# A block-diagonal state for one tile shape in linear attention, and a new order of jobs, in a fused mixer kernel on one core

## The chip, the core and the metric

The kernel runs on one core of a Trainium2 chip. The core has a matrix engine (TensorE, PE in the rows; its weight loads are PEld), a vector engine (DVE), a scalar engine (ACT), GpSimd (POOL) and SyncE (SP), which here only issues transfers. Each engine works through its own queue in order. The metric is the device time of one execution in microseconds (us); smaller is better.

## The reference

Three layers follow one another, for a batch B of 2 and a sequence S of 768. Inputs are float32, the weights are float64.

```python
# 1: linear attention with decay, 8 heads of D = 64
state = gamma * state + einsum('bhd,bhe->bhde', k[:, :, t], v[:, :, t])
y[:, :, t] = scale * einsum('bhd,bhde->bhe', q[:, :, t], state)
# 2: Fourier mixing, then a normalised MLP of 512 -> 2048 -> 512
u = x + real(fft(fft(x, axis=1), axis=2))
un = (u - mean(u)) / sqrt(var(u) + 1e-6)
x = u + relu(un @ w_ch1) @ w_ch2
# 3: 512 -> 1024, a gate from a convolution over 3 tokens, 1024 -> 512
h = relu(x @ w_in)
out = (h * sigmoid(conv3(h)) @ w_out)
```

## The kernel before

The whole program is a list of small jobs, one string `ORDER`. Each engine gets its instructions in the order of that string; nothing is reordered afterwards, so a job that waits holds everything behind it on the same engine. The names that matter here:

- Attention works on 12 tiles n of 128 tokens, 0 to 5 for the first batch, 6 to 11 for the second. `Lk`, `Lq`, `Lv` load one input tile each (256 KB, from the SP queue unless `ACT_LOADS` names it). `V` scales v by the decay (POOL, DVE if in `V_DVE`, ACT if in `V_ACT`). `K` and `Q` transpose k and q on PE, and ACT copies them out. `S` makes the scores on PE, and DVE masks them (L265). `A` adds the tile to the state (L276), and ACT copies the sums out (L279). `O` makes the output: the product with the state of the tiles before (L299), then the product of scores and v (L302); ACT copies it out. `X` transposes it back (L312), and DVE scales it to rows (L317); from the fourth tile of a batch on, SP writes the rows to DRAM as well.
- Fourier mixing: `F` and `G` fold each row block (two small instructions each; `F` on POOL unless in `FOLD_DVE`, `G` on DVE). `b0.0` to `b0.9` are the butterflies over the six blocks of a batch, 14 instructions of 128x512 (DVE, some on POOL unless in `FLY_DVE`). `t` transforms over tokens and `p` over features on PE; `m` and `r` add the results to u; `rev` gathers rows back from DRAM (POOL queue).
- `s`, `n`, `x` are the moments, the centring and the transposes of the MLP's input. `U00.f` and `D00.f` are its up and down products for batch 0, first half of the tokens, chunk f; `h` and `P` are the third layer's products.
- Weights arrive as float64 halves of chunks, 48 in all: `f` fetches 512 KB into one of three raw buffers, `d` decodes it to float32 with three DVE instructions (L507, L509, L511), `e` splits it into two parts (ACT L501; L503 on POOL if in `LOW_POOL`, else DVE).

The tile shapes on PE, rows by columns of the array: transposes and all MLP products use 128x128, the scores 64x128 (two heads in the two halves of the rows), the state 128x64 (two heads in the two halves of the columns), the product with the state 64x64, the value product 128x64. The state of the eight heads lies in a PSUM bank as 128 x 256: head 2hp+j in partitions 64j to 64j+63, columns 64hp to 64hp+63.

Of the kernel before, what the change touches and what calls it, by code (L numbers as in the profile page):

```python
# [42 lines left out]
ORDER = """
clear warm Lk0 ident K0 Lq0 Q0 masks S0 Lv0 V0 A0 Lk2 K2 Lq1 Q1 Lk1 K1 Lv1 V1 Lq2 Lv2 V2 O0 Lq3 Lq6 S1 Lk3 Q2 Lq4 A1
X0 F0 G0 O1 A2 Lv3 V3 S2 K3 Q3 X1 Q4 F1 G1 O2 A3 S3 Lk4 K4 Lk5 K5 Lv4 V4 X2 F2 S4 Lq5 Q5 Lk6 Lv6 V6 G2 Lv5 V5 Lv7 V7
f1 Lk7 Lq7 O3 K6 A4 X3 Q6 Lq8 F3 S5 f0 d1 Lk8 G3 b0.0 b0.3 O4 K7 X4 Q7 F4 S7 Lq9 G4 O5 X5 Q8 A6 A7 K8 F5 O7 d0 e0 G5
b0.2 b0.5 S6 O6 b0.1 b0.8 b0.9 b0.4 b0.6 b0.7 f2 d2 e1 Lk10 K10 f5 d5 tables t0.4 t0.0 t0.1 f3 d3 e2 rev0 e3 S8 t0.2
f4 d4 f6 d6 t0.3 p0.2 p0.0 m0.0 s00.0 n00.0 m0.2 p0.1 m0.1 s00.1 n00.1 s00.2 x00.0 X7 e6 n00.2 x00.1 x00.2 f8 e5 e4 f7
d7 Lk9 Lv8 V8 A8 Lk11 X6 Q9 K9 r0.0 U00.0 s01.0 r0.1 U00.1 s01.1 n01.1 d8 dev00 rec00 n01.0 Lv10 D00.0 U00.3 Lq10 Q10
F6 G6 Lv9 V9 x01.0 O8 Lv11 V11 K11 A9 f9 e7 r0.2 s01.2 dev01 rec01 U00.2 S9 x01.1 D00.1 V10 n01.2 x01.2 Lq11 O9 A10  # L50
f10 d10 e8 F7 G7 f11 d11 e11 U01.1 X9 F9 X8 F8 Q11 D00.2 D00.3 Z00.4.2 Z00.4.1 d9 e9 S10 U01.0 f23 U01.3 O10 f13 d13
f12 e10 d12 f15 G8 D01.0 Z00.4.0 U01.2 e12 d15 e15 G9 X10 F10 G10 b1.1 S11 D01.1 D01.2 U00.5 U00.4 e13 f14 d14 O11
b1.0 b1.3 f16 d16 f17 f18 D00.4 X11 F11 D01.3 Z01.4.0 Z01.4.2 b1.4 U00.6 G11 b1.2 U01.4 Z01.4.1 e14 d17 f20 e16 d18
f19 b1.5 D00.5 D00.6 Z00.7.0 U00.7 Z00.7.2 U01.5 Z00.7.1 b1.8 b1.9 b1.6 b1.7 e18 d19 f21 e17 d20 f22 D01.4 D01.5 U00.8
U01.6 t1.2 e20 d21 f24 t1.1 t1.0 e19 d22 e22 e21 d23 t1.4 D01.6 Z01.7.1 Z01.7.0 U00.9 t1.3 D00.7 D00.8 p1.1 rev1 d24
e24 m1.1 p1.2 m1.2 r1.2 f26 r1.1 Z01.7.2 U00.11 U00.10 d26 f31 e23 D00.9 U00.12 e26 f27 d27 e27 f25 d25 e25 f28 d28
D00.10 D00.11 U00.13 p1.0 e28 m1.0 s10.0 r1.0 s11.0 U01.7 D00.12 D00.13 U01.9 U01.8 n10.0 f32 s10.2 n10.2 f29 d29 e29
d31 e31 s10.1 D01.7 U01.10 s11.2 f30 d30 e30 D01.8 U01.11 d32 s11.1 D01.9 U01.12 D01.10 D01.11 U00.14 U00.15 x10.0
n10.1 dev11 rec11 f33 d33 D00.14 D00.15 Z00.16.2 Z00.16.1 U01.14 U01.13 x10.1 x10.2 n11.1 f38 f39 f36 n11.0 conv
Z00.16.0 dev10 rec10 D01.12 D01.13 D01.14 U10.2 U10.0 U10.1 D10.0 D10.1 U01.15 U10.3 D01.15 Z01.16.1 Z01.16.2 U10.5  # L60
Z01.16.0 x11.0 D10.2 U10.4 D10.3 U10.7 x11.1 n11.2 D10.4 D10.5 U10.6 U10.10 D10.6 U10.8 D10.7 D10.8 U10.9 U10.13 D10.9
D10.10 U10.11 U10.12 D10.11 U10.15 x11.2 D10.12 U11.2 D10.13 U10.14 y00.0 y00.1 D10.14 D10.15 Z10.16.0 Z10.16.1
Z10.16.2 U11.0 U11.1 D11.0 e33 d39 e32 d36 f34 U11.3 f35 D11.1 D11.2 e36 d34 e34 d35 U11.4 U11.5 D11.3 U11.7 D11.4
U11.6 e39 d38 e38 f37 d37 e37 f42 d42 y00.2 D11.5 D11.6 e42 D11.7 U11.10 U11.8 U11.9 e35 f40 d40 e40 f44 d44 f41 d41
e44 e41 D11.8 D11.9 U11.12 U11.11 f46 d46 f45 d45 e45 D11.10 U11.13 D11.11 h00.0 f47 d47 e47 f43 d43 e43 e46 D11.12
D11.13 U11.15 U11.14 y01.0 y01.1 y01.2 D11.14 D11.15 Z11.16.1 Z11.16.2 Z11.16.0 h01.0 c0.0 a0.0 h01.1 h00.1 c0.1 h01.2
h00.2 c0.2 h00.3 w0.0 y10.0 a0.2 w0.2 a0.1 h00.5 y10.1 h00.4 h01.3 c0.3 w0.1 h01.5 c0.5 a0.3 h01.4 c0.4 a0.4 h00.6
h01.7 y10.2 w0.4 w0.3 h00.7 y11.0 y11.1 y11.2 h01.6 c0.6 a0.5 w0.5 h10.2 a0.6 w0.6 h10.0 c0.7 a0.7 h10.1 w0.7 h11.1
c1.1 h11.0 c1.0 a1.0 w1.0 h10.3 h11.2 c1.2 a1.2 h11.6 w1.2 h10.6 P0.2 P0.3 a1.1 w1.1 h10.4 h11.3 c1.3 a1.3 w1.3 h10.7
h11.7 h11.4 c1.4 a1.4 c1.6 a1.6 h10.5 h11.5 P0.1 P0.4 c1.5 a1.5 P0.0 w1.5 w1.4 w1.6 c1.7 P0.5 a1.7 w1.7 P1.1 P1.0 P1.2  # L70
P1.4 P1.3 P1.5
"""


# [709 lines left out]
```

## Time and profile before

| | |
|---|---|
| Time, median of 3 runs | 528.16 us (527.57 to 528.64) |
| Time of the profiled execution | 527.51 us |
| Span of the profiled execution | 525.6 us (1.9 us of its time lie around the span) |
| PE busy | 506.1 us, 96% of the span |
| DVE busy | 322.9 us, 61% |
| ACT, POOL busy | 172.0 us, 66.0 us |
| Chain that ended last | 93% PE, 3% DVE, 1% DMA |

The span runs from the first instruction to the last. Engine time is how long the engine had an instruction at work; the chain is the work that ended last, followed back from the end. The shares are means over the whole span; the rows further down take single stretches of it.

### The profile page before, as it was taken

The page shows a single profiled execution, that of the slowest core. Times are in us where ns is not written, and L with a number is a line of the kernel's source. Part 1 is how long each engine was busy: PE and PEld are TensorE (multiplying, and loading weights), DVE is VectorE, ACT ScalarE, POOL GpSimd, SP SyncE. Part 2 cuts the span into 40 slices and gives each one's busy share as a digit, 9 for nine tenths or more (in the row PEclk, how much of TensorE's full clock was granted, in tenths as well). Part 3 has the DMA queues.
Part 4 walks back from the last instruction along what each step waited for, and adds up shares of the span by engine and source line. Part 5 has one row for each costly group of instructions (what it writes and reads, how often), then busy time and mean ns, then how long its engine had stood idle before and what let it go on. Part 6 is the DMA issues. An engine that isn't in the chain of part 4 may idle for free.

```text
span 525.6 us, 7790 instructions
## 1 busy us (share of the span) xinstructions
PE 506.1 (96%) x3182; PEld 453.9 (86%) x3182; DVE 322.9 (61%) x576; ACT 172.0 (33%) x336; POOL 66.0 (13%) x66
## 2 busy tenths in 40 slices
...
GB/s 194 204 239 257 179 103 81 162 96 87 174 107 143 157 104 58 126 76 2 0 1 0 1 0 1 148 94 134 67 2 0 1 1 1 41 0 61 40 40 61
DMA packets 60951, 42.59 MB, mean 81 GB/s; under 512 B 42098, under 2 KB 55026, under 8 KB 60916
## 3 DMA queue, kind: packets, MB, share of 16 engines
...
q8 instruction: 25, 0.41, 0.3%
...
q14 instruction: 10, 0.08, 0.1%
...
## 4 chain that ended last, share of the span: by engine, by line
PE 93%; DVE 3%; DMA 1%; ACT 1%; SPq 1%; issue 0%; ACTq 0%
PE h L136 9%; PE ac L136 9%; PE h L138 9%; PE h L137 9%; PE ac L138 9%; PE ac L137 8%; PE hi L138 4%; PE hi L137 4%; PE hi L136 4%; PE po L136 4%; PE po L138 4%; PE po L137 4%; PE sc L263 2%; PE px L302 2%; PE tr L579 2%; PE px L299 2%
## 5 line engine op out<-in xcount | busy, mean ns | idle before, releaser
L609 DVE SCALAR_TENSOR_TENSOR h<-h,h 128x384 fp32r<-128x384 f32 x64 | 35.2, 554 | 88.9 <-ACT h L608 88.9
L136 PE MATMUL ac<-wt,h 128*128 128x512 f32 x192 | 76.9, 400 | 0.0
L608 ACT ACTIVATE h<-h 128x384 fp32r<-128x384 f32 x64 | 31.2, 490 | 137.4 <-PE h L138 132.6
L138 PE MATMUL ac<-wt,h 128*128 128x512 f32 x192 | 75.8, 395 | 0.0
L137 PE MATMUL ac<-wt,h 128*128 128x512 f32 x192 | 75.5, 393 | 0.0
L503 POOL TENSOR_TENSOR wt<-word,wt 128x512 fp32r<-128x512 f32 x18 | 23.3, 1296 | 227.4 <-ACT wt L501 227.4
L501 ACT CAST wt<-word 128x512 fp32r<-128x512 f32 x48 | 29.0, 619 | 56.3 <-DVE word L511 53.7
L138 PEld LDWEIGHTS ac<-wt,h 128*128 128x128 f32 x192 | 36.1, 188 | 8.6 <-DVE h L609 0.3
L136 PEld LDWEIGHTS ac<-wt,h 128*128 128x128 f32 x192 | 36.1, 188 | 7.0 <-issue 0.3
L137 PEld LDWEIGHTS ac<-wt,h 128*128 128x128 f32 x192 | 36.1, 188 | 6.7
L136 PE MATMUL po<-wt,g 128*128 128x512 f32 (+1 forms) x104 | 39.1, 376 | 0.0
L138 PE MATMUL po<-wt,g 128*128 128x512 f32 (+1 forms) x104 | 39.0, 375 | 0.0
L137 PE MATMUL po<-wt,g 128*128 128x512 f32 (+1 forms) x104 | 39.0, 375 | 0.0
L667 DVE SCALAR_TENSOR_TENSOR cv<-hb,cw,cv 128x768 f32<-128x768 f32 x32 | 32.5, 1017 | 10.5 <-ACT cv L665 9.9
L511 DVE SCALAR_TENSOR_TENSOR word<-raw,word 128x512 int32<-128x512 int32 x48 | 34.6, 721 | 1.6
L509 DVE SCALAR_TENSOR_TENSOR word<-raw,word 128x512 int32<-128x512 int32 x48 | 33.7, 703 | 1.6
L507 DVE TENSOR_SCALAR word<-raw 128x512 int32<-128x512 int32 x48 | 21.6, 450 | 8.1 <-POOL wt L503 7.7
L696 DVE COPY ob<-po 128x512 f32<-128x512 f32 (+1 forms) x13 | 8.3, 648 | 29.4 <-PE po L138 29.4
L503 DVE TENSOR_TENSOR wt<-word,wt 128x512 fp32r<-128x512 f32 x30 | 20.4, 688 | 8.9 <-ACT wt L501 8.7
L138 PEld LDWEIGHTS po<-wt,g 128*128 128x128 f32 x104 | 19.5, 188 | 3.8
L137 PEld LDWEIGHTS po<-wt,g 128*128 128x128 f32 x104 | 19.6, 188 | 3.7
L136 PEld LDWEIGHTS po<-wt,g 128*128 128x128 f32 x104 | 19.5, 188 | 3.7
...
## 6 DMA issues: line engine op xcount, KB each, us to landing
...
```

The lines of the kernel that those rows point to most:

```text
L136: nc.tensor.matmul(o, ah, bh, start=start, stop=False)
L137: nc.tensor.matmul(o, ah, bl, start=False, stop=False)
L138: nc.tensor.matmul(o, al, bh, start=False, stop=stop)
L263: nc.tensor.matmul(ps[j][:, sl], kt[rows, sl], qt[rows, sl], start=True, stop=True)
L501: nc.scalar.copy(wt[:, 0, j], f32(word))
L503: eng.tensor_tensor(wt[:, 1, j], f32(word), f32(wt[:, 0, j]), op=ALU.subtract)
L507: nc.vector.tensor_scalar(word, raw[:, :, 1], 3, 0x3FFFFFF8, op0=ALU.logical_shift_left, op1=ALU.bitwise_and)
L509: nc.vector.scalar_tensor_tensor(word, raw[:, :, 1], -0x40000000, word, op0=ALU.bitwise_and, op1=ALU.bitwise_or)
L511: nc.vector.scalar_tensor_tensor(word, raw[:, :, 0], 29, word, op0=ALU.logical_shift_right, op1=ALU.bitwise_or)
L608: nc.scalar.activation(h2[:, 0], ps[:, :HB], AF.Relu)
L609: nc.vector.scalar_tensor_tensor(h2[:, 1], ps[:, :HB], 0.0, f32(h2[:, 0]), op0=ALU.max, op1=ALU.subtract)
L667: nc.vector.scalar_tensor_tensor(cv, hb[:, j:j + S], f32(cw[:, j * NF2 + f:j * NF2 + f + 1]), cv, op0=ALU.mult, op1=ALU.add)
```

## The change

The state is stored block-diagonally: for each pair of heads a 128 x 128 block in which head j fills rows and columns 64j to 64j+63, and the rest is zero, set once at the start (one more clearing instruction, on POOL). The product with the state then takes all 128 rows of q and the zeros fall out, so `A`, and both products of `O`, use the shape 128x64. ACT copies the state out in two instructions in place of one. The states take the place of one work buffer, which moves to the last of the spare tiles, and the q tiles of the second batch have one buffer in place of two.

The order is new throughout, and with it the lists that say which engine takes a job. Two loads (`q0`, `v1`) go out from the ACT queue in place of one. The fetches `f2` and `f0` stand behind six input tiles; seven fetches stand ahead of `Lv5`, where there was none. The part of the new and old order up to the last attention job is shown; the rest (second half of the first MLP and the third layer) is regrouped in the same way.

```diff
-V_ACT = ()
+V_ACT = (4,)
 V_DVE = (5, 6, 10)
-FOLD_DVE = (0, 9)
-FLY_DVE = ((0, 0), (0, 1), (0, 2), (0, 8))
-BACK_DVE = ((0, 2), (1, 0))
-LOW_POOL = (0, 3, 6, 7, 9, 12, 15, 18, 24, 27, 30, 31, 33, 36, 38, 39, 42, 45)
-WORD_BANK = (5, 37, 43)
-CENTRE_ACT = ((0, 0, 0), (0, 0, 2), (0, 1, 0), (0, 1, 2), (1, 0, 0), (1, 0, 2), (1, 1, 0))
-ACT_LOADS = ('k0',)
+FOLD_DVE = (0, 3, 5, 10)
+FLY_DVE = ((0, 0), (0, 1), (0, 8), (1, 8))
+BACK_DVE = ((1, 0),)
+LOW_POOL = (0, 3, 6, 7, 9, 12, 14, 15, 16, 18, 24, 25, 27, 30, 31, 33, 36, 39, 42, 43)
+WORD_BANK = (5, 19, 40, 45, 47)
+CENTRE_ACT = ((0, 0, 0), (0, 0, 2), (0, 1, 0), (0, 1, 2), (1, 0, 1), (1, 0, 2))
+ACT_LOADS = ('q0', 'v1')
 ORDER = """
-clear warm Lk0 ident K0 Lq0 Q0 masks S0 Lv0 V0 A0 Lk2 K2 Lq1 Q1 Lk1 K1 Lv1 V1 Lq2 Lv2 V2 O0 Lq3 Lq6 S1 Lk3 Q2 Lq4 A1
-X0 F0 G0 O1 A2 Lv3 V3 S2 K3 Q3 X1 Q4 F1 G1 O2 A3 S3 Lk4 K4 Lk5 K5 Lv4 V4 X2 F2 S4 Lq5 Q5 Lk6 Lv6 V6 G2 Lv5 V5 Lv7 V7
-f1 Lk7 Lq7 O3 K6 A4 X3 Q6 Lq8 F3 S5 f0 d1 Lk8 G3 b0.0 b0.3 O4 K7 X4 Q7 F4 S7 Lq9 G4 O5 X5 Q8 A6 A7 K8 F5 O7 d0 e0 G5
-b0.2 b0.5 S6 O6 b0.1 b0.8 b0.9 b0.4 b0.6 b0.7 f2 d2 e1 Lk10 K10 f5 d5 tables t0.4 t0.0 t0.1 f3 d3 e2 rev0 e3 S8 t0.2
-f4 d4 f6 d6 t0.3 p0.2 p0.0 m0.0 s00.0 n00.0 m0.2 p0.1 m0.1 s00.1 n00.1 s00.2 x00.0 X7 e6 n00.2 x00.1 x00.2 f8 e5 e4 f7
-d7 Lk9 Lv8 V8 A8 Lk11 X6 Q9 K9 r0.0 U00.0 s01.0 r0.1 U00.1 s01.1 n01.1 d8 dev00 rec00 n01.0 Lv10 D00.0 U00.3 Lq10 Q10
-F6 G6 Lv9 V9 x01.0 O8 Lv11 V11 K11 A9 f9 e7 r0.2 s01.2 dev01 rec01 U00.2 S9 x01.1 D00.1 V10 n01.2 x01.2 Lq11 O9 A10
-f10 d10 e8 F7 G7 f11 d11 e11 U01.1 X9 F9 X8 F8 Q11 D00.2 D00.3 Z00.4.2 Z00.4.1 d9 e9 S10 U01.0 f23 U01.3 O10 f13 d13
-f12 e10 d12 f15 G8 D01.0 Z00.4.0 U01.2 e12 d15 e15 G9 X10 F10 G10 b1.1 S11 D01.1 D01.2 U00.5 U00.4 e13 f14 d14 O11
-b1.0 b1.3 f16 d16 f17 f18 D00.4 X11 F11 D01.3 Z01.4.0 Z01.4.2 b1.4 U00.6 G11 b1.2 U01.4 Z01.4.1 e14 d17 f20 e16 d18
+clear warm Lq0 ident Lk0 K0 Q0 masks S0 Lv1 Lv0 Lk1 Lq1 V0 A0 K1 Q1 O0 f2 f0 Lk2 d2 d0 S1 K2 X0 Lq3 F0 G0 V1 O1 A1 Lv3
+e2 X1 V3 Lq2 Q2 S2 Lk3 K3 Q3 Lv2 V2 O2 A2 f1 d1 Lv6 V6 F1 f5 d5 Lk4 e0 Lv4 V4 X2 F2 S3 O3 f3 d3 G1 K4 Lq4 Q4 Lq5 Lq6
+G2 Lk5 A3 f6 Lk7 Lk6 f4 X3 F3 G3 Q6 Lq7 S4 b0.0 b0.3 Lv7 Lv5 Lk8 e3 d6 A4 tables Q5 K5 V7 e1 d4 O4 K7 S5 V5 K6 X4 Q7
+Lq8 F4 S7 G4 O5 A6 Lk9 K8 X5 F5 G5 b0.2 A7 Lk10 f10 S6 O6 K9 f7 b0.5 b0.1 b0.8 b0.9 b0.4 b0.6 b0.7 Q8 S8 Lq9 e4 d7 O7
+e6 e5 X6 Q9 t0.0 t0.3 t0.2 t0.1 t0.4 p0.1 m0.1 p0.0 m0.0 s00.0 s00.1 n00.0 n00.1 Lv10 f8 Lv9 V9 p0.2 m0.2 s00.2 Lv8 V8
+A8 O8 A9 f11 x00.0 n00.2 x00.1 X7 Lk11 K10 x00.2 rev0 Lv11 V11 S9 F6 Lq10 Q10 Lq11 K11 r0.1 s01.1 n01.1 U00.0 r0.2
+s01.2 U00.1 r0.0 s01.0 dev01 rec01 n01.0 V10 S10 F7 e7 G7 U00.2 x01.0 x01.1 n01.2 d11 f13 dev00 rec00 d8 f9 G6 e8 d10
+D00.0 D00.1 D00.2 e11 f15 O10 O9 A10 U00.3 x01.2 e10 X8 F8 Q11 d9 e9 f12 G8 X9 F9 D00.3 Z00.4.0 Z00.4.1 U01.0 U01.1 G9
+X10 F10 G10 b1.1 U01.2 Z00.4.2 d12 e12 f23 d13 S11 d15 e15 b1.4 b1.0 D01.0 D01.1 D01.2 U00.5 U01.3 U00.4 O11 f16 d16
+b1.3 f14 f20 e13 d14 f18 D00.4 U00.6 X11 F11 G11 b1.2 D01.3 Z01.4.1 Z01.4.2 Z01.4.0 U01.4 e14 d18 f24 b1.5 e16 d20 f17
...
-    sums = [states[:, 0, i * 256:(i + 1) * 256] for i in range(2)]
+    sums = [states[:, i, :].rearrange("p (a e) -> p a e", a=NP) for i in range(2)]
...
-    parts = [p[:, i, :] for p in parts for i in range(4)] + [states[:, 1, :]]
+    spare = [slot(9, [P, 4, H, D], "spare0"), uslot(1, 1, [P, 3, H, D], "spare1", F32)]
+    parts = [p[:, i, :] for p in parts for i in range(4)] + [spare[1][:, 2].rearrange("p h d -> p (h d)")]
...
-        return spare[6 + n % 2] if n >= NC else kv_late[4 + n % 2]
+        return spare[6] if n >= NC else kv_late[4 + n % 2]
...
+        nc.gpsimd.memset(states[:, 1, :], 0.0)
...
-                nc.tensor.matmul(st[j * D:(j + 1) * D, hp * D:(hp + 1) * D], k_tile(n)[:, 2 * hp + j, :],
+                nc.tensor.matmul(st[j * D:(j + 1) * D, hp * P + j * D:hp * P + (j + 1) * D], k_tile(n)[:, 2 * hp + j, :],
...
-        nc.scalar.copy(sums[(c + 1) % 2], st[:, 0:256])
+        for j in range(2):
+            sl = slice(j * D, (j + 1) * D)
+            nc.scalar.copy(sums[(c + 1) % 2][sl, :, sl], st[sl, :].rearrange("p (a e) -> p a e", a=NP)[:, :, sl])
...
-                rows = slice(j * D, (j + 1) * D)
-                nc.tensor.matmul(place(h), sums[c % 2][rows, hp * D:(hp + 1) * D], qt[rows, hp * P:(hp + 1) * P],
+                nc.tensor.matmul(place(h), sums[c % 2][:, hp, j * D:(j + 1) * D], qt[:, hp * P:(hp + 1) * P],
```

## Rows read from the trace of the kernel before

**Rows 1.** Windows of 10 us: length, busy us of PE, PEld, DVE, ACT, POOL (instructions), clock, DMA.

```profile
40.00:50.00 10.00, 7.81 (x118) 6.28 (x116) 8.01 (x14) 3.78 (x9) 3.58 (x4) 1.00 0.80 226
50.00:60.00 10.00, 5.03 (x32) 4.51 (x29) 9.62 (x16) 2.44 (x5) 3.01 (x3) 0.79 0.62 207
70.00:80.00 10.00, 4.76 (x33) 3.97 (x33) 9.15 (x22) 4.28 (x9) 4.04 (x4) 0.81 0.38 97
80.00:90.00 10.00, 10.00 (x65) 9.16 (x64) 7.60 (x16) 5.34 (x10) 3.41 (x4) 0.85 0.52 107
```

**Rows 2.** Timeline: last butterfly; first mix; last centring; first up product.

```profile
55.81 0.69 DVE L383 TENSOR_TENSOR fold<-fold,fold 128x512 f32<-128x512 f32 x1
...
70.66 0.43 DVE L457 TENSOR_TENSOR mix<-pc,mix 128x258 f32<-128x258 f32 x1 [0.35 <-ACT mix L434]
...
78.64 0.72 ACT L556 ACTIVATE un<-u,ve 128x512 f32<-128x512 f32 x1 [2.75 <-DVE ve L535]
...
83.53 0.42 PE L136 MATMUL h<-un00h,wt 128*128 128x384 f32 x1
```

**Rows 3.** Chain that ended last, 20 to 32 us: start us, us, engine and line.

```profile
20.90 1.02 PE px L299 x16
21.92 1.02 PE px L302 x16
22.94 0.47 PE st L276 x16
23.41 1.09 PE sc L263 x16
...
30.27 0.61 PE st L276 x16
...
31.47 0.44 PE pq L252 x4
```

**Rows 4.** The page's groups of a decode: count | busy us, mean ns | idle before.

```profile
L511 DVE SCALAR_TENSOR_TENSOR word<-raw,word 128x512 int32<-128x512 int32 x48 | 34.6, 721 | 1.6
L509 DVE SCALAR_TENSOR_TENSOR word<-raw,word 128x512 int32<-128x512 int32 x48 | 33.7, 703 | 1.6
L507 DVE TENSOR_SCALAR word<-raw 128x512 int32<-128x512 int32 x48 | 21.6, 450 | 8.1 <-POOL wt L503 7.7
```

**Rows 5.** Timeline: a fold; a decode and a state copy beside POOL; two masks.

```profile
16.44 0.42 DVE L336 TENSOR_TENSOR eod<-u 128x256 f32<-128x256 f32 x1
...
43.20 1.10 DVE L509 SCALAR_TENSOR_TENSOR word<-raw,word 128x512 int32<-128x512 int32 x1
43.20 0.37 ACT L279 COPY states<-st 128x256 f32<-128x256 f32 x1
...
43.71 1.17 POOL L336 TENSOR_TENSOR eod<-states 128x256 f32<-128x256 f32 x1
...
48.16 1.29 DVE L265 TENSOR_TENSOR work<-sc,mask 128x512 f32<-128x512 f32 x2
```

**Rows 6.** Windows: inputs alone; the lowest with inputs queued; weights and tables alone.

```profile
10.00:11.00 1.00, 0.61 (x6) 0.40 (x5) 0.09 (x1) 0.99 (x2) 0.00 (x0) 1.00 1.36 217
24.00:26.00 2.00, 2.00 (x24) 1.71 (x21) 1.29 (x3) 0.88 (x2) 0.40 (x1) 1.00 0.91 164
48.00:52.00 4.00, 2.24 (x24) 1.45 (x20) 3.86 (x7) 1.56 (x4) 1.27 (x1) 1.00 1.00 376
```

**Rows 7.** PE timeline: the sixth input tile arrives.

```profile
10.80 0.41 PE L252 MATMUL pk<-ident,xin 128*128 128x128 f32 x2 [0.39 <-DMA xin<-in_k_dram]
```

**Rows 8.** Window of the first token transforms; then one transform's first weight load, and the next's.

```profile
56.50:62.50 6.00, 5.95 (x28) 5.95 (x29) 5.79 (x10) 1.70 (x4) 1.08 (x2) 0.50 0.77 221
...
64.49 0.30 PEld L403 LDWEIGHTS g<-tabs,fold 128*128 128x128 f32 x2
...
65.82 0.30 PEld L403 LDWEIGHTS g<-tabs,fold 128*128 128x128 f32 x2
```

**Rows 9.** Window over the up and down products beside attention's rest.

```profile
84.00:204.00 120.00, 120.00 (x804) 108.17 (x803) 102.58 (x190) 39.66 (x89) 31.16 (x29) 1.00 0.41 126
```

More of the change, by code (lines that the diff above doesn't have):

```diff
@@ L54 @@
[L54 to L68, printed above, removed]
@@ L69 @@
-c1.1 h11.0 c1.0 a1.0 w1.0 h10.3 h11.2 c1.2 a1.2 h11.6 w1.2 h10.6 P0.2 P0.3 a1.1 w1.1 h10.4 h11.3 c1.3 a1.3 w1.3 h10.7
-h11.7 h11.4 c1.4 a1.4 c1.6 a1.6 h10.5 h11.5 P0.1 P0.4 c1.5 a1.5 P0.0 w1.5 w1.4 w1.6 c1.7 P0.5 a1.7 w1.7 P1.1 P1.0 P1.2
-P1.4 P1.3 P1.5
+clear warm Lq0 ident Lk0 K0 Q0 masks S0 Lv1 Lv0 Lk1 Lq1 V0 A0 K1 Q1 O0 f2 f0 Lk2 d2 d0 S1 K2 X0 Lq3 F0 G0 V1 O1 A1 Lv3
+e2 X1 V3 Lq2 Q2 S2 Lk3 K3 Q3 Lv2 V2 O2 A2 f1 d1 Lv6 V6 F1 f5 d5 Lk4 e0 Lv4 V4 X2 F2 S3 O3 f3 d3 G1 K4 Lq4 Q4 Lq5 Lq6
+G2 Lk5 A3 f6 Lk7 Lk6 f4 X3 F3 G3 Q6 Lq7 S4 b0.0 b0.3 Lv7 Lv5 Lk8 e3 d6 A4 tables Q5 K5 V7 e1 d4 O4 K7 S5 V5 K6 X4 Q7
@@ new lines @@
+X10 F10 G10 b1.1 U01.2 Z00.4.2 d12 e12 f23 d13 S11 d15 e15 b1.4 b1.0 D01.0 D01.1 D01.2 U00.5 U01.3 U00.4 O11 f16 d16
+b1.3 f14 f20 e13 d14 f18 D00.4 U00.6 X11 F11 G11 b1.2 D01.3 Z01.4.1 Z01.4.2 Z01.4.0 U01.4 e14 d18 f24 b1.5 e16 d20 f17
+rev1 D00.5 D00.6 Z00.7.0 U01.5 U01.6 Z00.7.1 b1.8 b1.9 b1.6 b1.7 Z00.7.2 e18 d17 f22 e20 d24 f19 D01.4 D01.5 U00.9
+U00.8 t1.1 e17 d23 f21 D01.6 Z01.7.2 Z01.7.1 Z01.7.0 U00.7 d19 f26 e23 d21 f25 t1.2 t1.4 t1.0 t1.3 e19 e21 d22 e22
+D00.7 p1.1 D00.8 D00.9 m1.1 r1.1 U00.10 U00.11 e24 p1.2 s10.1 n10.1 d26 e26 d25 e25 f27 d27 D00.10 D00.11 U01.7 U00.12
@@ new lines @@
+e27 m1.2 r1.2 s11.2 U00.13 f32 conv f30 d30 f29 d29 D00.12 U01.8 D00.13 p1.0 e29 m1.0 s10.0 r1.0 n10.0 e30 U01.11 f33
+f31 d31 e31 D01.7 D01.8 U01.9 U01.10 s10.2 dev10 rec10 D01.9 D01.10 D01.11 f28 d28 e28 U01.14 U00.14 U00.15 x10.0
+n10.2 D00.14 D00.15 Z00.16.1 Z00.16.0 f34 d34 s11.0 U01.13 U01.12 f38 x10.1 x10.2 n11.0 n11.2 d32 f39 D01.12 U10.3
+s11.1 dev11 rec11 Z00.16.2 D01.13 U10.0 D01.14 U10.1 D10.0 D10.1 U10.2 U10.4 D10.2 D10.3 U10.9 U10.5 D10.4 D10.5 U10.6
+U01.15 x11.0 n11.1 D10.6 U10.7 x11.1 D01.15 Z01.16.0 Z01.16.2 U10.8 Z01.16.1 x11.2 D10.7 U10.12 D10.8 D10.9 U10.10
```

13 lines of the change are left out of this document (11 added, 2 removed).

## The prediction

> **What bounds the kernel now.** The table of the profile says PE almost throughout, and the chain agrees; that is a mean. I read next the windows of 10 us, to find where PE is not the bound. From 83 us to the end of the products it never idles, so a change there pays only by taking PE work away. Ahead of that it idles in two holes: 5.0 of the 10 us from 50, 5.2 of the 10 us from 70, with 2.2 more from 40; in both holes DVE is over 90% busy, and the granted clock is 0.79 to 0.85 up to 90 us [rows 1]. So the time is that at which the first up product U00.0 can start (83.5 us, [rows 2]), plus the PE work still left then, plus a tail that the change leaves alone. I price the change by those two terms.
>
> The first hole is the butterflies on DVE: PE waits for the last of them, which ends at 56.5 [rows 2]. The second is the chain mix, moments, centring: 8.7 us from the first mix at 70.66 to the last centred block at 79.36 [rows 2], in which DVE works and PE has little queued.
>
> **Part 1, the shapes.** The chain early on is pure PE, so a piece's length there is its cost [rows 3]. The state sums take 0.47 behind the value product, which has their shape, but 0.61 behind another shape; the state product takes 1.02 and the value product behind it 1.02 again, although 16 records of 128 columns at 2.4 GHz need 0.85. So a change of shape costs 0.14 to 0.17; I take 0.155. Counted from the two strings (job by job, with the shape of each), PE changes shape 62 times before and 46 times after: ten of the sixteen fall between the two products of O, six come from the regrouping.
>
> The wider product costs nothing else: at 64x64 and at 128x64 the 16 records take the same 1.02 [rows 3], because successive heads alternate between two column halves in either form. The Trainium skill (TensorEngine Tiling, Tiling Modes) gives a 64x64 array four independent tiles and a 128x64 array two, so by it the old shape could have gone twice as fast and the change would lose up to 0.43 us in each of ten products; the equal rows say that this kernel never had more than two in flight, and by the rows the difference in the sum is nothing.
>
> ACT copies the state twice. One copy of 128x256 takes 0.37 [rows 5]; the two halves cost between nothing and 0.37 more per A, and I take 0.37, on an engine under 55% busy in these windows [rows 1], one or more jobs ahead of the O that needs it. The extra clearing on POOL lies ahead of the first input. V4 on ACT (eight instructions, at most 8 x 0.37 = 3.0 us by the same row) has the time until A4. These three at nothing; without cover, at most 0.4 us per tile.
>
> **Part 2, the work left at U00.0.** Left in the old order behind U00.0: seven transposes (Q10, K11, Q11, X8 to X11), two A, three S, four O, and 20 changes of shape. Bare of changes these cost 0.44, 0.47, 0.94 and 1.74 each (the last two less their changes) [rows 3]: 3.1 + 0.9 + 2.8 + 7.0 = 13.8, and 20 x 0.155 = 3.1, together 16.9 us. In the new order: five transposes, one A, two S, three O, 8 changes: 2.2 + 0.5 + 1.9 + 5.2 + 1.2 = 11.0 us. So **5.9 us** of PE work has gone from behind U00.0, into the holes ahead of it or altogether.
>
> **Part 3, when U00.0 starts.** Here the order of DVE decides. Durations: a decode 0.45 + 0.70 + 0.72 = 1.87, call it 1.9 [rows 4]; masks 1.29; F or G two of 0.42, call it 0.77 (they overlap) [rows 5]; every other 128x512 instruction 0.69 to 0.72 [rows 2, 4].
>
> Transfers first. Inputs alone flow at 217 GB/s, weights and tables alone at 376 [rows 6]. So an input tile (262 kB) takes 1.2 us and a fetch (524 kB) 1.4. The bytes of six inputs and the constants were there at 10.8 before [rows 7]; behind the same bytes f2 is visible at 12.1 or so, f0 at 13.5. Going on so through the new order, Lk2 is visible at 14.7, f1 at 22.2, f5 at 24.8, f3 at 28.6, f6 at 34.8, Lv5 at 42.2. SP's holds lie within that: f5, f3, f6 and f4 each wait for a raw buffer (d2, d0, d1, d5), Lq7 for Q6 (one q buffer now), and all later loads, Lv5 among them, queue behind.
>
> DVE then: d2 12.1 to 14.0, d0 to 15.9, masks S1 to 17.2 (PE done at 13.5: the mask is late by d2 and d0, and O1 waits for it); X0, F0, G0, e2, X1 to 20.9; S2 to 23.2 (waits for PE, whose K2 was late); d1, V6, d5, X2, S3 to 29.7; d3, G1, G2, X3, F3, G3, S4 to 36.7; b0.0, b0.3, d6, e1, d4, S5 to 43.9; V5, X4, S7, G4 to 47.4; X5, F5, G5, S6 to 51.0; the last 11 butterfly instructions of 0.72 to **58.9**. Five decodes more than in the old order stand ahead of the last butterfly, so the transforms start 2.4 us later than before, although DVE no longer idles early.
>
> It comes back behind. PE now has K9, Q8, S8, O7, X6, Q9 (some 5 us) in the first hole, so I expect the full clock for the transforms: before, they ran at 0.50 until 62.5; at full clock one takes 65.82 - 64.49 = 1.33 [rows 8], so five take 6.7, to 65.6. No decode but d7 is left in DVE's way there. The first mix follows 2.6 later (p0.1 with its copies; before it was 70.66 less 67.15, which is 64.49 and two transforms more, with decodes between), the last centred block 8.7 behind it: 76.9. A8, O8, A9 fill 3.1 us of the second hole. x00.2, S9, Q10, K11 (0.6 + 1.1 + 0.9) end at 79.5. That walk leaves out what POOL does to DVE: beside POOL's fold a decode instruction took 1.10 in place of 0.70 [rows 4, 5], 0.8 us per decode. Bounds: none of the eight decodes is stretched (79.5), or all (85.9); POOL was busy 30 to 40% of the windows from 40 [rows 1], so three: 2.4. U00.0 at **81.9**, 1.6 earlier than before.
>
> Sum: 1.6 + 5.9 = 7.5 us. 527.5 - 7.5 = 520.0 for a profiled execution; the median of the runs shown lies 0.65 above, so **520.7**. This case's own range is 518 to 525 (stretch as above; if the clock is at 0.50 again for half of the transforms, 3 us more).
>
> **Rivals.**
> *Inputs late, by half.* If fetches flow between the two rates, DVE waits at d1, d5, d3, f6 and V5 in turn; Lv5 has 1.7 us of slack in the walk. Half of the mechanism below gives 524 to 527.
>
> *Inputs late: slower.* Place: SP's queue up to Lv5, 10.4 MB including X3's rows. If fetches move no faster than inputs (217 GB/s), Lv5 is visible at 51, V5 and with it O5, X5 and the butterflies are 7.0 late; with 2 us more from SP's holds U00.0 stands at 91 and the time is near 530. It decides from U00.0 at 89.4 (81.9 + 7.5), that is Lv5 later than about 51. For it: one window with inputs queued fell to 164 [rows 6], and decodes stand ahead of masks. Against it: the inputs' 217 come with a DMA share of 1.36 and the weights' 376 with 1.00, so these differ in kind.
>
> *DVE gives it back.* From 84 to 204 us DVE is busy 102.6 of 120 us [rows 9]. With PE 7.5 us ahead the same work is 91% of what is left. It has room, but if up and down products wait for decodes in places, up to the 5.9 us are lost: 522 to 527.
>
> *The wide product loses its pairs.* Then each of ten products takes 0.85 longer; the three behind U00.0 cost 2.6, all ten 8.5: 523 to 529. The value product of the same shape speaks against it [rows 3].
>
> *The change of shape costs nothing* and only the order counts: 16 x 0.155 = 2.5 less, 523.
>
> **How the numbers follow.** Chances: forecast, with the last rival, 0.60; inputs late by half 0.14; slower 0.13; DVE gives it back 0.11; wide product 0.02. About 0.2% (1 us) is what a measurement can tell from no change. Faster 0.60 + 0.13 + 0.08 + 0.01 = 0.82; slower 0.13; the same 0.05. The range: below, DVE's waits in the walk (2.0 ahead of d2, 1.0 at S2) might vanish and no decode be stretched, which gives 515.3, and I stop at 516; above it takes in both middle rivals, to 527.5. That leaves out the slower case and little else.
>
> **What the changed profile would show.** Right: no pause between L299 and L302, the pair in 1.9 us; U00.0 between 79 and 86; token transforms at clock 1.00 from 59 on; both holes mostly filled; no PE idle behind. PE idle moved into the first 45 us, in front of masks that wait for decodes. Wrong: V5 waiting for Lv5 beyond 44 us with DVE idle; U00.0 behind 86; PE waiting for L503 or L501 between 84 and 200; more than 2.1 us for O's two products.

## The result and the profile after

The changed kernel takes 518.38 us (median of 4 runs, 518.10 to 519.01), the kernel before 527.87 on the same chip (4 runs): ratio 0.982, 95% interval 0.9803 to 0.9837. The profiled execution took 518.22 us with a span of 516.4, so 9.2 us of span have gone; 520.7 was forecast, 516 to 527.5 the range. PE busy fell from 506.1 to 499.8 us.

The windows that answer to [rows 1]:

```profile
40.00:50.00 10.00, 8.47 (x122) 7.32 (x122) 9.23 (x17) 4.46 (x10) 2.45 (x3) 1.00 0.94 255
50.00:60.00 10.00, 7.73 (x98) 6.55 (x98) 9.44 (x17) 4.24 (x11) 1.27 (x1) 1.00 0.77 216
70.00:80.00 10.00, 8.64 (x119) 7.69 (x118) 8.95 (x21) 6.98 (x17) 3.61 (x5) 1.00 0.63 159
80.00:90.00 10.00, 10.00 (x72) 9.40 (x73) 8.59 (x23) 6.10 (x14) 6.78 (x7) 1.00 0.12 29
```

PE's idle time in the two holes is 2.3 and 1.4 us in place of 5.0 and 5.2, and the clock is whole in all four. The milestones, as in [rows 2] (last butterfly, first mix, last centring, first up product):

```profile
60.12 0.69 DVE L385 TENSOR_TENSOR fold<-fold,fold 128x512 f32<-128x512 f32 x1
...
69.48 0.43 DVE L459 TENSOR_TENSOR mix<-pc,mix 128x258 f32<-128x258 f32 x1 [3.76 <-ACT mix L436]
...
77.47 0.72 ACT L558 ACTIVATE un<-u,ve 128x512 f32<-128x512 f32 x1 [0.16 <-DVE ve L537]
...
80.77 0.42 PE L136 MATMUL h<-un00h,wt 128*128 128x384 f32 x1
```

The last butterfly comes 4.3 us later than before, since five decodes more stand ahead of it; the transforms, at full clock, make up for it, and U00.0 starts 2.8 us earlier. Behind U00.0 lie 516.4 - 80.8 = 435.6 us of span, before 442.1: 6.4 less. The transforms, the stretch behind U00.0 and the early transfers are each one window (answering to [rows 8], [rows 9] and [rows 6]):

```profile
60.87:67.60 6.73, 6.73 (x60) 6.73 (x61) 4.75 (x8) 3.63 (x9) 2.53 (x3) 1.00 0.98 254
84.00:204.00 120.00, 120.00 (x761) 109.32 (x761) 105.12 (x193) 39.11 (x86) 31.72 (x28) 1.00 0.37 111
8.00:12.00 4.00, 4.00 (x66) 3.45 (x63) 2.30 (x4) 2.22 (x5) 0.25 (x1) 1.00 1.14 310
```

PE idles nowhere in the 120 us, though DVE is 88% busy there. The chain shows the change of shape (start us, us, engine and line):

```profile
86.28 0.38 PE h L136
...
95.69 1.02 PE px L301 x16
96.72 0.87 PE px L304 x16
97.59 0.87 PE px L301 x16
98.46 0.87 PE px L304 x16
```

Two `O` stand one behind the other here. The first state product, behind another shape, takes 1.02; everything after it in the same shape 0.87. So one change costs 0.15, as put. `h` (an up product) at 86.28 stands behind scores; the `h` pieces behind it take 0.17, so a change in front of these products costs 0.2.

### The profile page after: what moved, and what is told of

Same layout as the page of the kernel before. It is cut to its first block, busy times and chain, and to the rows that moved or that the text cites. A ratio compares the mean times of both kernels' runs of the same rounds, so it can differ in the third digit from the quotient of the medians.

```text
span 516.4 us, 7838 instructions
## 1 busy us (share of the span) xinstructions
PE 499.8 (97%) x3182; PEld 450.7 (87%) x3182; DVE 327.1 (63%) x578; ACT 177.1 (34%) x353; POOL 66.3 (13%) x64
## 4 chain that ended last, share of the span: by engine, by line
PE 89%; DVE 5%; DMA 3%; SPq 1%; ACT 1%; issue 1%; POOL 0%; ACTq 0%; DVEq 0%
PE h L136 9%; PE h L138 9%; PE ac L136 9%; PE ac L138 9%; PE h L137 9%; PE ac L137 9%; PE hi L137 4%; PE hi L138 4%; PE hi L136 4%; PE po L137 4%; PE po L138 4%; PE po L136 4%; PE tr L581 2%; DMA xin<-in_k_dram 1%; DMA eod<-in_q_dram 1%; PE px L301 1%
## 5 line engine op out<-in xcount | busy, mean ns | idle before, releaser
L505 POOL TENSOR_TENSOR wt<-word,wt 128x512 fp32r<-128x512 f32 x20 | 26.8, 1344 | 211.8 <-ACT wt L503 211.8
L509 DVE TENSOR_SCALAR word<-raw 128x512 int32<-128x512 int32 x48 | 23.7, 494 | 6.2 <-DMA raw<-in_moe_w_in_dram 3.0
```

The lines of the kernel that those rows point to most:

```text
L505: eng.tensor_tensor(wt[:, 1, j], f32(word), f32(wt[:, 0, j]), op=ALU.subtract)
L509: nc.vector.tensor_scalar(word, raw[:, :, 1], 3, 0x3FFFFFF8, op0=ALU.logical_shift_left, op1=ALU.bitwise_and)
```

## The experiments

The theory: the gain is PE work moved from behind U00.0 into holes that DVE makes, with DVE's queue setting U00.0's start; the shape is worth a small part. Rivals: the shape is the main part; the early weights do not matter because inputs feed PE; a transfer, not DVE, sets the start. Ratios below are against the kernel before; where single stretches are compared, the numbers are those of the profiled executions.

How far one execution can be trusted is seen from three runs below (the hole left empty, the same with POOL free, the hole filled idly), which keep the order of the changed kernel up to the last butterfly: there it comes at 61.59, 59.43 and 59.59, against 60.12, with K2 starting at 15.20, 13.81 and 15.06, against 15.05. So a microsecond at the last butterfly or at U00.0, between single executions, need not come from an edit. Behind U00.0 they agree far better: 435.6 to 435.7 us in the changed kernel and in six of the runs below.

**Old shapes in the new order.** The state is 128x256 again, `A`'s copy one instruction, the state product 64x64.

```diff
-    sums = [states[:, i, :].rearrange("p (a e) -> p a e", a=NP) for i in range(2)]
+    sums = [states[:, i, 0:256] for i in range(2)]
...
+                rows = slice(j * D, (j + 1) * D)
-                nc.tensor.matmul(place(h), sums[c % 2][:, hp, j * D:(j + 1) * D], qt[:, hp * P:(hp + 1) * P],
+                nc.tensor.matmul(place(h), sums[c % 2][rows, hp * D:(hp + 1) * D], qt[rows, hp * P:(hp + 1) * P],
```

> The new order with the state and its product in their old shapes (128 x 256 state, one copy, product at 64x64). PE changes shape 58 times in place of 46, eight of the twelve ahead of U00.0 and four behind. Theory (most of the gain is the order, a change of shape costs 0.15 to 0.2 us where PE is the bound): 0.6 to 0.8 us behind U00.0 and 0 to 1.6 ahead, so 519.0 to 520.8. Rival (the shapes are the main part of the gain): 523 or more. Rival (the old shape ran its products at least as well, the wide product costs PE time): 518 or less.

Measured: 519.34 us, ratio 0.9832 (0.9811 to 0.9853); span 518.0; U00.0 at 81.74. By medians the shape is worth 1.0 us, but the interval overlaps that of the changed kernel, so this is not clear of nothing. What is clear stands behind U00.0: 436.3 us in place of 435.6, the four changes of shape at 0.155. The chain of this run has the same two `O`, now with a change in front of each product:

```profile
96.66 1.02 PE px L300 x16
97.68 1.02 PE px L303 x16
98.70 1.02 PE px L300 x16
99.73 1.02 PE px L303 x16
```

U00.0 is 1.0 later as well, but K2 starts 0.4 later in this execution (15.42), and PE then runs at half clock until 21 us (in the changed kernel until 18.6), so that microsecond can't be put down to the shape.

**New shapes in the old order.** The new shapes put into the kernel before. The second state takes the place of a work buffer, as in the change; the last spare tile goes to a tile that is used only later.

```diff
-    sums = [states[:, 0, i * 256:(i + 1) * 256] for i in range(2)]
+    sums = [states[:, i, :].rearrange("p (a e) -> p a e", a=NP) for i in range(2)]
...
-    spare = [spare[0][:, i] for i in range(4)] + [spare[1][:, i] for i in range(3)]
+    spare = [spare[0][:, i] for i in range(4)] + [spare[1][:, i] for i in range(2)]
+    spare.append(u[1][0][:, 2, :].rearrange("p (h d) -> p h d", h=H))
```

> The old order with the new shapes; room for the second state is made in a tile that is not yet in use, so that no load moves. 52 changes of shape in place of 62, six fewer ahead of U00.0, four fewer behind. Theory: 0.6 to 0.8 us less behind U00.0, 0 to 1.2 less ahead of it, where DVE sets the pace: 526 to 527.3. Rival (the shapes are the main part): 523 or less. Rival (a second copy per state delays what follows on ACT): 528 or more.

Measured: 527.35, ratio 0.9987 (0.9974 to 1.0001), a gain of 0.7 that is not clear of nothing; U00.0 at 83.38, 0.15 earlier. The chain has the pair of products at the place of [rows 3]:

```profile
21.06 1.02 PE px L302 x16
22.09 0.87 PE px L305 x16
```

Only the second row changed, 1.02 to 0.87, under the same order: the price of the change of shape, and that the wide product costs nothing, stand alone here. It hardly pays: six of the ten `O` stand ahead of U00.0, where PE waits for DVE later anyway, and the four behind are 0.6 us by the chain's rows. This execution shows nothing even of these (442.2 us behind U00.0, 442.1 before), because its clock comes back later. The windows of this run and of the kernel before:

```profile
84.00:85.00 1.00, 1.00 (x5) 1.00 (x4) 0.86 (x2) 0.35 (x1) 0.00 (x0) 0.50 1.04 238
84.00:85.00 1.00, 1.00 (x7) 1.00 (x6) 0.97 (x3) 0.44 (x1) 0.00 (x0) 1.00 0.66 152
```

Half clock from U00.0 at 83.4 to 85 us costs 0.8, about what the shape gives. By medians order and shape together gain 9.5, the order alone 8.7, so the order is the main part.

**First weights behind the first inputs.**

```diff
-O0 f2 f0 Lk2 d2 d0 S1
+O0 Lk2 S1
...
-Lv3 e2 X1
+Lv3 X1
...
-O2 A2 f1 d1 Lv6
+O2 A2 f2 f0 f1 d2 d0 e2 d1 Lv6
```

> The new kernel with f2 and f0 moved from behind O0 to behind A2, and d2, d0, e2 moved to just ahead of d1; all else as it is. Theory (DVE sets the pace up to the butterflies, so its idle time in the first 20 us is worth filling): K2 no longer waits (2.4 us), the inputs land 2.8 us earlier, but 4.5 us of DVE work stand later; U00.0 0.5 to 3 us later, 519 to 521.5. Rival (the early fetch holds up the inputs and costs more than it brings): 516 to 518.

Measured: 523.63, ratio 0.9909 (0.9892 to 0.9925); U00.0 at 86.31, last butterfly at 65.66, both over 5 us later than in the changed kernel: the early fetches, with the decodes they feed, give more than half of the gain (5.2 of 9.5), far more than expected. Windows and PE's timeline of this run:

```profile
10.00:20.00 10.00, 8.70 (x120) 7.35 (x118) 5.16 (x10) 4.72 (x11) 3.18 (x4) 1.00 0.91 200
30.00:40.00 10.00, 6.07 (x47) 5.03 (x48) 7.83 (x16) 4.75 (x15) 1.41 (x2) 0.55 1.19 253
...
33.93 2.57 PE L304 MATMUL px<-work,xin 128*64 128x128 f32 x16 [7.78 <-DVE work L266]
```

From 10 to 20 us DVE is busy 5.16 us; in the changed kernel it is 7.81. The decodes d2 and d0 and the split e2, which it could have done there, now stand with d1 and d5 ahead of S3's masks, so PE waits 7.78 us and the clock is at 0.55 from 30 to 40. The 5.2 us are thus the idle time, the place where the decodes went and the clock together; no run tells them apart. In the changed kernel DVE's queue has hardly a gap from 21.6 us to the last butterfly, so what is not done early has no free time later.

**The second hole left empty.** The twelve attention jobs between V8 and U00.0 go back behind U00.1.

```diff
-V8 A8 O8 A9 f11
+V8 f11
...
-X7 Lk11 K10 x00.2 rev0 Lv11 V11 S9 F6 Lq10 Q10 Lq11 K11 r0.1
+X7 x00.2 rev0 F6 r0.1
...
-s01.2 U00.1 r0.0
+s01.2 U00.1 A8 O8 A9 Lk11 K10 Lv11 V11 S9 Lq10 Q10 Lq11 K11 r0.0
```

> The new kernel with A8, O8, A9, K10, S9, Q10, K11 and the loads among them moved from the second hole to behind U00.1. Theory (the gain is PE work taken from behind U00.0 into time in which PE waits for the chain of mix, moments and centring): 4.9 us of work and four changes of shape (0.6 to 0.8) stand behind U00.0 again; U00.0 is about 2.1 us earlier, since S9, Q10, K11 no longer stand between x00.2 and it; net 3.4 to 3.6 us slower, near 522. Rival (the hole is short because of the clock and the early decodes, and what fills it does not matter): within 1 us of the new kernel.

Measured: 530.28, ratio 1.0041 (1.0026 to 1.0055): slower than before the change. One thing in POOL's timeline is a mishap of the edit:

```profile
94.33 1.04 POOL L247 TENSOR_TENSOR spare<-spare,decay 128x512 f32<-128x512 f32 x1 [15.04 <-DMA spare<-in_v_dram]
```

V11's scaling waits 15 us for its load, and the additions to u stand behind it in POOL's queue. So the same again with POOL free (K10 to V10 now behind n01.0, K11 behind U00.2, Lq10 left early; the line that receives them is shown):

```diff
-n01.0 V10 S10 F7 e7 G7 U00.2 x01.0
+n01.0 A8 O8 A9 Lk11 K10 Lv11 S9 Q10 Lq11 V10 S10 F7 e7 G7 V11 U00.2 K11 x01.0
```

> The new kernel with A8, O8, A9, K10, S9, Q10 moved behind U00.1 and K11 behind U00.2, as in the run before, but with Lq10 left early and V11 behind V10 on POOL's queue, so that POOL does not wait for Lv11 ahead of r0.0 (it stood still for 15.0 us there, and the buffers of the up products with it). Theory (PE work taken from behind U00.0 into the second hole): 4.9 us and four changes of shape stand behind U00.0 again, U00.0 is about 2.1 us earlier, net 3.4 to 3.6 us slower than the new kernel: near 522. Rival (the loss of the run before was the hole itself, not POOL's wait): 527 or more. Rival (what fills the hole does not matter): within 1 us of 518.4.

Measured: 529.26, ratio 1.0024 (1.0011 to 1.0037), span 526.5. That is 10.9 more than the changed kernel by medians, where 3.4 to 3.6 were expected, so freeing POOL gave back only 1.0. Windows of this run:

```profile
70.00:80.00 10.00, 4.22 (x29) 3.05 (x27) 8.98 (x20) 4.17 (x10) 7.19 (x8) 0.97 0.25 75
80.00:90.00 10.00, 9.34 (x72) 8.71 (x71) 5.02 (x15) 2.84 (x5) 1.34 (x2) 0.69 0.09 21
90.00:100.00 10.00, 8.20 (x83) 7.37 (x84) 5.70 (x13) 6.02 (x15) 2.29 (x2) 1.00 0.27 62
```

U00.0 does start 1.3 us earlier (79.45), but 0.7 of that was there at the last butterfly (59.43), ahead of what the edit moves, so the edit bought 0.6 of the 2.1 expected. All the rest is worse: 5.6 us of work put behind it (three transposes, one `S`, one `O`, two `A`: 4.9 bare by [rows 3], and four changes of shape), 2.5 of PE idle from 80 to 100, and, the clock being at half for 6.2 of the 10 us from 80, some 3.1 lost to it. Together -1.3 + 5.6 + 2.5 + 3.1 = 9.9, against 526.5 - 516.4 = 10.1. What the expectation left out are the last two terms: the waits of the moved jobs, and the clock.

To tell the clock from the rest, the hole of the last run was filled with four idle products (128x512 each, whose results nothing reads):

```diff
+    def fill():
+        ps = bank("fill")
+        nc.tensor.matmul(ps, ident, tabs[:, 0:512], start=True, stop=True)
...
-p0.2 m0.2
+p0.2 fill0 fill1 m0.2
...
-X7 x00.2
+X7 fill2 fill3 x00.2
```

> The kernel of the last run on the hole (attention's jobs behind U00.1, POOL free) with four matmuls of 128x512 put into the second hole, two behind p0.2 and two behind X7, whose results nobody reads: extra work, nothing left out. Theory (an unfilled hole costs twice: the work stands behind U00.0, and the clock falls to 0.50 in it and stays there for some 6 us of full queue, 3.1 us of work): the clock stays at 1.00 through 90 us, and the span falls by 2.5 to 3.5 us against that run's 526.5, to 523 to 524. Rival (the clock is a symptom, the loss is only work and waits behind U00.0): 526 or more.

Measured: 528.97, ratio 1.0010 (0.9995 to 1.0025). That is 0.3 less by medians, and the intervals of the two runs overlap, so no gain is shown; 523 to 524 was expected and the rival's 526 or more came. The span of the profiled execution is 525.6, only 0.9 less. Its window:

```profile
80.00:90.00 10.00, 8.19 (x71) 7.70 (x71) 5.66 (x18) 3.80 (x7) 1.39 (x2) 0.83 0.13 29
```

The clock here is 0.83 in place of 0.69, so 1.4 of the 3.1 us was taken away, and in these two executions 0.9 came back; PE now idles 1.8 us in this window. By these sums the clock is the smaller part and the displaced work with its waits the larger. How much the 1.7 us left of the clock and the idle are worth by themselves stays open: no run here had the one without the other.

**Is it a transfer that sets the start?** In the changed kernel Q7's load waits for the one q buffer, and Q7 for it. A second buffer, and the load ahead of f4:

```diff
-        return spare[6] if n >= NC else kv_late[4 + n % 2]
+        return (u[1][0][:, 2, :].rearrange("p (h d) -> p h d", h=H), spare[6])[n % 2] if n >= NC else kv_late[4 + n % 2]
...
-Lk6 f4 X3 F3 G3 Q6 Lq7 S4
+Lk6 Lq7 f4 X3 F3 G3 Q6 S4
```

> The new kernel with a second q buffer for the second batch, in a tile that is used only later, and Lq7 issued ahead of f4 in place of behind X3's rows. Theory (DVE sets the pace from 21 to 61 us; PE's wait for Lq7, 0.8 us at 43, is hidden behind it): U00.0 within 0.6 us, 517.7 to 518.5. Rival (the chain through Lq7, Q7, S7, O5, X5 sets the pace there): 2 us earlier, 516 to 517.

Measured: 518.07, ratio 0.9813 (0.9799 to 0.9827); U00.0 at 80.78, last butterfly at 60.13, as in the changed kernel. PE's wait is gone and nothing else, so the load of Q7 alone does not set the start.

**One decode twice.** d4 is done twice, so that DVE has 1.9 us more to do ahead of the butterflies.

```diff
         to_float32(word, raws[h])
+        if h == 4:
+            to_float32(word, raws[h])
```

> The new kernel with d4 decoded twice over, 1.9 us more of DVE ahead of S5, nothing else. Theory (DVE sets the pace up to the last butterfly; it stands idle for 0.6 us between X4 and X5): the last butterfly and U00.0 are 1.2 to 1.9 us later, 519.5 to 520.3. Rival (PE or the loads set the pace there): 518.4 to 518.8.

Measured: 520.93, ratio 0.9856 (0.9839 to 0.9873): 2.55 more than the changed kernel. The profiled execution is the longest of its four (522.45), with the last butterfly at 64.32 and U00.0 at 84.96, both 4.2 later than in the changed kernel. That is more than the edit. PE's timeline, then DVE's, at the decode itself:

```profile
16.10 1.09 PE L253 MATMUL pk<-ident,xin 128*128 128x128 f32 x4 [3.43 <-DMA xin<-in_k_dram]
...
41.76 0.42 DVE L511 TENSOR_SCALAR word<-raw 128x512 int32<-128x512 int32 x1
...
44.27 1.19 DVE L511 TENSOR_SCALAR word<-raw 128x512 int32<-128x512 int32 x1
```

d6 starts at 41.76, at 40.03 in the changed kernel: 1.7 of the delay are there before the decode that was doubled. K2's input came 1.0 later in this execution, and PE then ran at half clock from 16 to 22 us. The edit itself is 1.9 and the 0.77 by which d4's first instruction (1.19) is stretched: 2.7, near the 2.55 of the medians. The median lies above the 519.5 to 520.3 expected; by the two ratios (0.9856 and 0.982) the difference is 1.9 us, with some 1.3 either way. So work put into DVE's queue does delay U00.0, by about its own length. That a shorter queue would bring it forward does not follow; the next runs ask that.

**Can DVE be relieved?** Four orders move e1 and d4 behind the butterflies. The first, by itself:

```diff
-V7 e1 d4 O4
+V7 O4
...
-S8 Lq9 e4 d7
+S8 Lq9 e1 d4 e4 d7
```

> The new kernel with e1 and d4 (2.6 us of DVE) moved from ahead of S5 to behind S8, into the 3.8 us in which DVE waits for the first mix. Theory in its plain form (DVE alone sets the pace): the last butterfly ends 2.6 us earlier, U00.0 likewise, 515.8. Theory with both chains tied (DVE and Lq7, Q7, S7, O5, X5 end within a microsecond of each other at X5): 0 to 0.8 us earlier, 517.6 to 518.4. Rival (the decode is not on the path): no change, and the later d4 delays U00.2: 518.4 to 519.

Measured: 521.16, ratio 0.9877 (0.9862 to 0.9892); last butterfly at 60.28, not earlier, first mix at 71.89, 2.4 later. DVE's timeline shows where the 2.6 us went, at V5 and X5:

```profile
45.36 0.78 DVE L247 TENSOR_TENSOR xin<-xin,decay 128x512 f32<-128x512 f32 x1 [2.23 <-DMA xin<-in_v_dram]
...
49.54 0.69 DVE L319 TENSOR_TENSOR states<-xr,decay 128x512 f32<-128x512 f32 x1 [0.44 <-PE xr L314]
```

V5 waits 2.2 us for the load Lv5, X5 0.4 for PE, whose chain comes through Q7 and its load. So DVE's queue, Lv5 and Q7 end close together ahead of the butterflies: with the first shortened the others hold.

The next has this edit and the second q buffer (Lv5 stays where it was):

> The two edits together. Theory with both chains tied: X5 at about 47.2 on DVE in place of 49.4, the last butterfly near 58.6 in place of 60.8, U00.0 2 to 2.5 us earlier: 515.8 to 516.4. Rival (PE, not DVE, is the bound there): as the run with two q buffers alone. Rival (neither is on the path): 518.4.

Measured: 520.10, ratio 0.9859 (0.9841 to 0.9878). The last butterfly is 1.0 earlier (59.15), where 2.2 were expected; K2 started 0.8 earlier in this execution (14.22), so how much of that is the edit's is open. V5 waits 1.55 for Lv5, and from 30 us to X5's transposes PE is the chain, which was a rival:

```profile
30.07:48.40 18.33, 17.60 (x224) 15.40 (x226) 14.45 (x27) 9.65 (x23) 3.98 (x5) 0.91 1.05 258
```

So PE's own work is a further chain close behind. The time is longer all the same, and ACT's timeline shows why:

```profile
63.58 0.62 ACT L503 CAST wt<-word 128x512 fp32r<-128x512 f32 x1 [8.23 <-DVE word L513]
```

e4 on ACT waits 8.2 us for d4, and behind it stand the transforms' copies (the first at 66.06, in the changed kernel at 62.28).

Then the second q buffer, Lv5 earlier, e1 again behind S8, d4 in the gap that the transforms leave DVE, and e4 behind it with its second half on POOL (4 added to `LOW_POOL`):

```diff
-Lv7 Lv5 Lk8
+Lv5 Lv7 Lk8
...
-Lq9 e4 d7 O7 e6 e5 X6 Q9
+Lq9 e1 d7 O7 e6 e5 X6 d4 Q9
...
-p0.0 m0.0 s00.0
+p0.0 m0.0 e4 s00.0
```

> The run with both edits mended: two q buffers and Lq7 early, Lv5 ahead of Lv7, e1 behind S8, d4 behind X6, and e4 behind m0.0 with its second half on POOL, so that ACT's copies of the transforms no longer queue behind e4. Theory (that run lost its gain to ACT, which stood still for 8.2 us on d4 with O7's copy and the transforms' copies behind it): the last butterfly ends about 1 us earlier than in the new kernel, the first mix too, U00.0 near 79.8: 517.0 to 517.6. Rival (the gap in which DVE waits for the first mix is of no use, what is put there delays mix): 518.4 or more.

Measured: 525.22, ratio 0.9951 (0.9939 to 0.9964). Last butterfly at 59.32 and first mix at 68.68, both 0.8 earlier, as planned, and U00.0 at 87.61. POOL's timeline and PE's grouped waits:

```profile
72.88 1.27 POOL L505 TENSOR_TENSOR wt<-word,wt 128x512 fp32r<-128x512 f32 x1 [11.73 <-ACT wt L503]
74.10 2.68 POOL L247 TENSOR_TENSOR spare<-spare,decay 128x512 f32<-128x512 f32 x2
...
PE st L277 <- POOL spare L247: 5.7, 1, 5.7
```

e4's second half on POOL waits for its first on ACT, and V9 and V8 stand behind it; the state sums on PE wait 5.7 us. Last, with e4 behind V8:

```diff
-p0.0 m0.0 e4 s00.0
+p0.0 m0.0 s00.0
...
-Lv8 V8 A8
+Lv8 V8 e4 A8
```

> The run before with one job moved: the split e4 stands behind the scalings V9 and V8 in POOL's queue instead of ahead of them. If its late start came from the state sums waiting for those scalings alone: PE waits for them under 2 us in place of 5.7, last butterfly 59.3 and first mix 68.7 stay, U00.0 between 79.8 and 80.8, time 517.0 to 518.2, at or below the changed kernel. Rival, the decode moved behind the butterflies is late for something else (its split on POOL stretches DVE's moments and centring, or the decode's raw buffer holds up fetches): U00.0 behind 81.5, time 519 or more.

Measured: 520.62, ratio 0.9873 (0.9847 to 0.9899). PE's wait for POOL is 0.7 us now and the first mix 0.7 earlier (68.76), so the queue was the cause of the 5.7. U00.0 is at 81.50 all the same. The timeline of this run:

```profile
69.36 2.49 POOL L247 TENSOR_TENSOR spare<-spare,decay 128x512 f32<-128x512 f32 x2 [8.13 <-DMA spare<-in_v_dram]
...
69.56 1.40 DVE L462 TENSOR_TENSOR u<-u,mix 128x512 f32<-128x512 f32 x1
...
70.88 0.41 DVE L459 TENSOR_TENSOR mix<-pc,mix 128x258 f32<-128x258 f32 x1
```

V9 came 3.2 us later than in the changed kernel (69.36 against 66.14), beside DVE's addition to u, which takes 1.40 in place of 0.69 there: that is the whole 0.7. The next split on POOL, at 75.15, does the same to the third addition (1.39), and U00.0 is 0.7 late. The rest of what this execution loses lies behind U00.0 (437.6 us against 435.6), in DVE's and PE's timelines:

```profile
84.20 0.69 DVE L533 BATCH_NORM_STATS2 bs<-u 128x6 f32<-128x512 f32 x1 [1.70 <-POOL u L471]
...
90.95 1.09 PE L581 MATMUL tr<-ident,un 128*128 128x128 f32 x8 [1.66 <-ACT un L558]
```

POOL's additions to u start 2.4 later than in the changed kernel (82.87 against 80.43), with the split ahead of them; DVE's moments wait for these, and PE for the centring. No version tried here is faster than the changed kernel by more than the measurement tells; the second q buffer (518.07) equals it.

## Why the prediction was right

*The sum.* 7.5 us were forecast, 9.2 of span came: U00.0 2.8 earlier (1.6 forecast), 6.4 less behind it (5.9). Both terms have the right sign and place; both were too small. The 1.2 of the first lies near the spread of single executions (59.4 to 61.6 at the last butterfly in one order).

*Part 1.* The change of shape at 0.155 is confirmed by the chains (1.02 and 0.87). Twelve of them were taken back in the new order: the four behind U00.0 are worth 0.6 us, those ahead of it nothing that can be told from the spread; the ten in the old order are worth 0.7 by medians, not clear of nothing. The last rival had its premise wrong (a change does cost time) and its conclusion nearly right: the order alone gives 8.7 of 9.5. The wide product cost nothing; ACT's two copies take 0.74, as forecast, and hold PE once, for 0.9 us, at A9 in the second hole; V4 on ACT holds nothing.

*Part 2.* The term was 0.5 too small. In front of the large products a change costs 0.2 (0.38 less 0.17) and not 0.155, but of the twelve changes fewer behind U00.0 only two stand there (six in the old order, four in the new), which makes 0.1; the other 0.4 stays open. The Trainium skill (TensorEngine Tiling (Array Packing), Key Properties) says that a change of the tiling mode drains the engine; the rows agree, with 0.15 to 0.2 us for each.

*Part 3.* The order of DVE was the right thing to walk: work added to it delays the start, as the doubled decode showed. But it was not alone; Lv5's load, Q7's chain and PE's own work end close behind it, and taking work out of it gained nothing. The walk put the last butterfly at 58.9 without POOL's stretch and the stretch at 2.4, together 61.3; it ended at 60.8. The groups of DVE over the first 61 us:

```profile
L509 DVE TENSOR_SCALAR word<-raw 128x512 int32<-128x512 int32 x7 | 3.7, 531 | 0.8 <-DMA raw<-in_moe_w_ch_dram 0.8
...
L505 DVE TENSOR_TENSOR wt<-word,wt 128x512 fp32r<-128x512 f32 x2 | 2.3, 1134 | 1.7 <-ACT wt L503 1.7
...
L337 DVE TENSOR_TENSOR eod<-u 128x256 f32<-128x256 f32 x1 | 1.1, 1068 | 0.0
L377 DVE TENSOR_TENSOR fold<-fold 128x512 f32<-128x512 f32 x1 | 1.0, 1012 | 0.0
```

Against 0.43, 0.68, 0.42 and 0.69 bare that is 0.7 + 0.9 + 0.65 + 0.3 = 2.6 us of stretch: the size forecast, but mostly on a split and a fold, and of the decodes' instructions only on the first. The 60.8 against 58.9 is a sum of four: d2 began 1.1 earlier (10.96 in place of 12.1), since inputs and the two fetches flowed together at 310 GB/s, between the rates of [rows 6]; the waits were 2.5 longer (3.5, most of it 1.0 ahead of X0 and 1.7 ahead of e2, in place of 1.0); the stretch is 2.6; and some 2.1 came back, because instructions follow one another more closely than the walk had it (d6 takes 1.78 to the start of the next, not 1.9). That the sum fits so well is in part luck. And from the transforms' end (67.4) to the first mix it is 2.0, not 2.6. The 0.5 at the butterflies and this 0.6 are the 1.1 us by which U00.0 was earlier than forecast. The rest holds: transforms 6.6 (6.7 forecast), first mix to last centred block 8.7 (8.7).

*The rivals.* Inputs late: K2 waited 2.4 us at 12.6, Q7 0.8 at 42.6, and no decode ahead of the butterflies waited for a fetch more than 0.8; the second buffer for q gained nothing. But the 1.7 us of slack that the walk gave Lv5 were not there. In the run with the hole empty and POOL free, with the same order up to this point, DVE's timeline has V5 waiting for it:

```profile
45.07 0.69 DVE L247 TENSOR_TENSOR xin<-xin,decay 128x512 f32<-128x512 f32 x1 [0.30 <-DMA xin<-in_v_dram]
```

That is 2.9 later than the walk's 42.2. In the changed kernel V5 starts at 45.53 without a wait, only because DVE's own queue was 1.6 late there; had DVE kept to the walk (43.9), it would have stood for Lv5 for about a microsecond. So this rival was nearer than its chance says, and that it cost so little was luck. DVE gives it back: no PE idle in the 120 us behind. But these dangers are small only in this very order: the runs that moved a few decodes or attention jobs lost 1.7 to 12 us, mostly by a queue. For what the early fetches and their decodes are worth (5.2 us) the prediction had no term; its walk contained it without saying so.
